# Narrow stationary blocks, four side by side, for the small fp32 products of a linear-attention and feed-forward kernel, and a later first load on ScalarE

## Chip, cores and metric

One core of a Trainium2 chip runs the kernel. The metric is device microseconds of one execution, as the median of several runs. TensorE (PE) multiplies, VectorE (DVE), ScalarE (ACT) and GpSimd (POOL) do the elementwise work, and SyncE (SP) issues most of the loads.

## Reference

For each of 4 batches and 4 heads (sequence 1088, head dimension 32, r = 8) there are quadratic features of queries and keys; the result feeds a feed-forward layer with 2048 hidden units on 4352 tokens of width 128.

```python
a = np.einsum('rd,bhsd->bhsr', S1, x); b = np.einsum('rd,bhsd->bhsr', S2, x)
phi(x) = np.einsum('bhsi,bhsj->bhsij', a, b).reshape(..., r * r)      # 64 features
kv  = np.einsum('bhsf,bhsd->bhfd', phi(k), v)
z   = np.sum(phi(k), axis=2)
x   = (phi(q) @ kv) / (phi(q) . z + 1e-06)        # heads side by side: 128 wide
h   = x @ w_in
g   = where(h >= 1, h, where(h <= -1, 0, (h + 1)**2 / 4))
out = g @ w_out
```

S1, S2, w_in and w_out are 64-bit floats; the kernel turns them into 32-bit parts on chip.

## The kernel before

**Attention, per batch.** The sequence is cut into 9 tiles of 128 tokens. `keys` projects each key tile onto S1 and S2 (`abk`, L432: the key tile is stationary, 128 columns, and the 64 columns of `s_all` move), copies it to SBUF (`ab`, L437), forms the features (`kp`, L442), and sums two things over the tiles in PSUM: the normaliser (`z`, L451: 32 stationary columns, 32 moving) and the key sums (`kv`, L468: two products of 64 stationary and 128 moving columns a tile). The normaliser's diagonal blocks are kept (`zm`, L456), multiplied back by S2 (L458, with `back` stationary) and put into `proj`. `kv` is masked, transposed and copied (`kvm`, L478, `kvb`). `queries` projects query tiles onto `proj` (`abq`, L497: 128 stationary, 96 moving), makes the features divided by the denominator (`as`, `terms`, `den`, `ap`, `qp`), transposes them (`tp`, L528) and gathers (`nd`, L542: two products of 64 stationary columns). `x_hi` and `x_lo` (L548) split the result in two parts for the feed-forward layer. All these products are in plain fp32: the trace has two records, called passes here, for each such matmul of the program (the transposes have one).

**Feed-forward, in 144 units** of up to 512 tokens by 128 hidden columns: three fp32r matmuls up (L584 to L586), an activation on ACT and DVE (L595, L597, L600, L606), a subtraction on POOL (L610), three matmuls down (L620, L621, L624). Each is 512 (or 256) moving columns against 128 stationary ones.

**The order** on each engine comes from `Plan`, which is run when the program is built: every step has a due time, an engine and an assumed cost; at each moment it takes the earliest due step that its own clock thinks is ready. Tile pools give buffers. Where PE has nothing to do before 24 us, it gets a filler: a bf16 product of 512 columns (`wide`, L279) or of 256 (`narrow`, L280). ScalarE issues one load itself, the first chunk of `w_in` (`raw_i`, L325).

Of the kernel before, what the change touches and what calls it, by code (L numbers as in the profile page):

```python
# [63 lines left out]
class Plan:  # L64
# [46 lines left out]
    def run(self):  # L111
# [26 lines left out]
        while left or done:  # L138
# [13 lines left out]
            for e in engines:  # L152
# [21 lines left out]
                    if best[2] is not None and now + best[1].ways[best[2]][1] > soon[1] + 0.05:  # L174
                        continue
                if e == "PE" and best is None and now < self.warm:
                    cost, filler = (0.115, self.narrow) if now > 2.5 else (0.43, self.wide)
                    f = Step(0.0, [("PE", cost, None, (), (), filler)])
                    f.taken, f.start = 0, now
                    order.append(f)  # L180
                    free_at[e] = now + cost
                    heapq.heappush(events, free_at[e])
                    continue
# [72 lines left out]
def tile_kernel(ctx: ExitStack, tc: tile.TileContext, qT, kT, v, S, w_in, w_out, outT):  # L256
# [32 lines left out]
        return Buf("ps", name, [P, 512])  # L289


    ident = cst.tile([P, P], F32, name="ident")
    make_identity(nc, ident)
    mask = cst.tile([P, 2, F], F32, name="mask")
    nc.gpsimd.memset(mask, 0.0)
    for h in range(H):
        nc.gpsimd.memset(mask[h * D : (h + 1) * D, h % 2], 1.0)
    blocks = cst.tile([HR, HR], F32, name="blocks")
    nc.gpsimd.memset(blocks, 1.0)
    nc.gpsimd.affine_select(out=blocks, in_=blocks, compare_op=ALU.is_ge, fill=0.0, base=0,  # L300
                            pattern=[[-R, H], [0, R]], channel_multiplier=1)
    nc.gpsimd.affine_select(out=blocks, in_=blocks, compare_op=ALU.is_ge, fill=0.0, base=R - 1,
                            pattern=[[R, H], [0, R]], channel_multiplier=-1)
# [12 lines left out]
    SC = S.shape[1]  # L316
    s_raw = cst.tile([P, SC, 2], I32, name="s_raw")
    s_all = cst.tile([P, SC], F32, name="s_all")
    back = cst.tile([HR, P], F32, name="back")
    proj = [cst.tile([P, H, 3 * R], F32, name=f"proj{i}") for i in range(2)]  # L320


# [55 lines left out]
            out=lo, in0=of(mag), in1=hi.bitcast(F32), op=ALU.subtract), r=[mag, toks[0]], w=[toks[1]])  # L378

    def weights(due, src, c, hi, lo, tag, due_load=None, lands=None):  # L380
        raw = Buf("raw", f"raw_{tag}{c}", [P, WC, 2], I32)
        load(due - 4 if due_load is None else due_load, src[:, c * WC : (c + 1) * WC, :], raw, P * WC * 8, lands=lands)
        w = slice(c * WC, (c + 1) * WC)
        from_double(due, lambda: of(raw), raw, WC, f"{tag}{c}", hi=hi[:, w], lo=lo[:, w],
                    toks=[(f"{tag}h", c), (f"{tag}l", c)])
# [28 lines left out]
    def keys(b, d):  # L414

        kb, qb, vb = loaded[b]
        front = b == 0
        tag = "h" if front else "at"
        late = 3.0 if front else 0.0
        z = bank(f"z{b}")  # L420
        kp = Buf("kp", f"kp{b}", [P, NTL, H * F])
        abs_ = []
        groups = GRP if front else [range(0, 5), range(5, NTL)]
        for gi, grp in enumerate(groups):
            n = len(grp)
            kt = [kb.part(gi) if front else kb]
            ab = bank(f"abk{b}_{gi}", tag)
            sbuf = Buf("ab", f"ab{b}_{gi}", [P, 2, 5 * H, R])

            def project(ab=ab, grp=grp):  # L430
                for i, t in enumerate(grp):
                    nc.tensor.matmul(of(ab)[:, i * 64 : (i + 1) * 64], lhsT=of(kb)[:, t], rhs=s_all.rearrange("p (c h i) -> p h c i", c=2, h=H),  # L432
                                     start=True, stop=True)

            plan.add(d(0.05 + 0.1 * gi), "PE", n * 0.22, project, r=[*kt, "s_all"], w=[ab])
            view = lambda ab=ab, n=n: of(ab)[:, : n * 64].rearrange("p (m c i) -> p m c i", c=2, i=R)
            plan.add(d(0.1 + 0.1 * gi), "ACT", act(n * 64), lambda sbuf=sbuf, view=view, n=n: nc.scalar.copy(  # L437
                of(sbuf)[:, :, : n * H].rearrange("p c m i -> p m c i"), view()), r=[ab], w=[sbuf])
            pool = front and gi in KP_POOL
            eng = nc.gpsimd if pool else nc.vector  # L440
            plan.add(d(0.15 + 0.1 * gi), "POOL" if pool else "DVE", pool_t(n * 256) if pool else dve(n * 256),
                     lambda sbuf=sbuf, view=view, n=n, grp=grp, eng=eng, pool=pool: eng.tensor_tensor(  # L442
                out=of(kp)[:, grp[0] : grp[-1] + 1].rearrange("p t (h i j) -> p (t h) i j", h=H, i=R),
                in0=of(sbuf)[:, 0, : n * H].unsqueeze(3).broadcast_to([P, n * H, R, R]),
                in1=(of(sbuf)[:, 1, : n * H] if pool else view()[:, :, 1]).unsqueeze(2).broadcast_to([P, n * H, R, R]), op=ALU.mult),
                r=[sbuf] if pool else [ab, sbuf], w=[kp.part(gi)])

            def zsum(sbuf=sbuf, n=n, grp=grp):
                for i, t in enumerate(grp):
                    m = slice(i * H, (i + 1) * H)  # L450
                    nc.tensor.matmul(of(z)[:HR, :HR], lhsT=of(sbuf)[:, 1, m], rhs=of(sbuf)[:, 0, m],  # L451
                                     start=(t == 0), stop=(t == NTL - 1))

            plan.add(d(0.16 + 0.1 * gi), "PE", n * 0.07 + 0.1, zsum, r=[sbuf], w=[z])
        zm = Buf("zm", f"zm{b}", [HR, HR])
        plan.add(d(0.45), "DVE", dve(32), lambda: nc.vector.tensor_tensor(  # L456
            out=of(zm), in0=of(z)[:HR, :HR], in1=blocks, op=ALU.mult), r=[z], w=[zm])
        plan.add(d(0.5), "PE", 0.3, lambda: nc.tensor.matmul(  # L458
            of(z)[:, 64 : 64 + HR], lhsT=back, rhs=of(zm), start=True, stop=True), r=[zm, "back"], w=[z])
        plan.add(d(0.55), "ACT", act(32), lambda: nc.scalar.copy(  # L460
            proj[b % 2][:, :, 2 * R :], of(z)[:, 64 : 64 + HR].rearrange("p (h i) -> p h i", h=H)),
            r=[z], w=[("proj", b % 2)])
        kv = bank(f"kv{b}")

        def sums(grp):
            for t in grp:
                for p in range(2):
                    nc.tensor.matmul(of(kv)[64 * p : 64 * p + 64, :P], lhsT=of(vb)[:, t, 64 * p : 64 * p + 64],  # L468
                                     rhs=of(kp)[:, t, p * P : (p + 1) * P], start=(t == 0), stop=(t == NTL - 1))

        for gi, grp in enumerate(groups):
            vt = [vb.part(0) if front else vb]
            plan.add(d(0.5 + 0.1 * gi) + late, "PE", len(grp) * 0.24 + 0.1, lambda grp=grp: sums(grp),
                     r=[kp.part(gi), *vt], w=[kv])
        kvm = Buf("kvm", f"kvm{b}", [P, 2, F])
        plan.add(d(0.8) + late, "DVE", dve(P), lambda: nc.vector.tensor_tensor(
            out=of(kvm), in0=of(kv)[:, :P].rearrange("p (s f) -> p s f", s=2), in1=mask, op=ALU.mult), r=[kv], w=[kvm])
        plan.add(d(0.85) + late, "PE", 0.11, lambda: nc.tensor.transpose(  # L478
            out=of(kv)[:, P : 2 * P], in_=of(kvm).rearrange("p s f -> p (s f)"), identity=ident), r=[kvm], w=[kv])
        kvb = Buf("kvb", f"kvb{b}", [P, P])  # L480
        copy_to(d(0.9) + late, lambda: of(kvb), lambda: of(kv)[:, P : 2 * P], P, [kv], [kvb])
        return kvb

    def queries(b, kvb, dues):
        _, qb, _ = loaded[b]
        front = b == 0
        for gi, grp in enumerate(QGRP[b]):
# [88 lines left out]
    def unit(u):  # L576
# [55 lines left out]
                     lat=P * n * 4 / 410e3)  # L632


    table = cst.tile([P, 1], F32, name="table")
    plan.add(-50, "ACT", 1.3, lambda: nc.scalar.copy(table, ones[:, :1]), w=["table"])
    load(-30, S, s_raw, P * SC * 8, tok="s_raw")
    load_attn(0, -29, [-28.5, -27], -27.5)
    from_double(-25, lambda: s_raw, "s_raw", SC, "s", whole=s_all, whole_tok="s_all")
    turned = bank("turned")  # L640
    plan.add(-13, "PE", 0.11, lambda: nc.tensor.transpose(
        out=of(turned)[:HR, :P], in_=s_all[:, HR:], identity=ident),
        r=["s_all"], w=[turned])
    plan.add(-13, "ACT", act(P), lambda: nc.scalar.copy(back, of(turned)[:HR, :P]), r=[turned], w=["back"])
# [7 lines left out]
    for u, (c0, n, j) in enumerate(units):  # L652
        first_unit.setdefault(j // JW, u)
    for c in range(DFF // WC):
        weights([I0, I1, first_unit[c] - 6][min(c, 2)], w_in, c, wi_hi, wi_lo, "i", *((None, None) if c else (-40, 4.6)))
        weights([O0, O1, first_unit[c] - 2][min(c, 2)], w_out, c, wo_hi, wo_lo, "o", None if c else -26)
    need = {}
    for b in range(1, B):
# [74 lines left out]
```

## Time and profile before

| | |
|---|---|
| median of 3 runs | 256.61 us (256.57 to 256.63) |
| the profiled execution | 257.05 us, of which the span is 254.9 us |
| granted TensorE clock, mean | 1.0 |
| busy share: PE, PEld, DVE, ACT, POOL | 98, 78, 77, 82, 74% |
| passes of abk, abq, kv, z in the trace | 72, 72, 144, 72 |
| feed-forward matmuls | 864 |

The span is the stretch from the first to the last instruction of the program; 2.15 us of the execution's time lie outside it. A busy engine in the profile may still be waiting within an instruction, and the ends of matmuls are modelled, so starts say more than durations there.

### The profile page before, as it was taken

How to read it: one execution, taken by the hardware profiler on the slowest of the kernel's cores; microseconds unless marked ns; L12 is line 12 of the kernel's file. 1: busy time of each engine (PE TensorE's matmuls, PEld its weight loads, DVE VectorE, ACT ScalarE, POOL GpSimd, SP SyncE). 2: the span in 40 equal slices, each digit the busy share in tenths (PEclk: the TensorE clock that was granted, in tenths of full speed). 3: DMA queues.
4: the chain of work that ended last, by engine and by line, in shares of the span. 5: the costliest groups of instructions: out<-in, count | busy, mean ns of one | idle time of the engine just before them, and what ended most of it. 6: DMA issues, size and time to landing. Idle time of an engine off the chain costs nothing.

```text
span 254.9 us, 4257 instructions
## 1 busy us (share of the span) xinstructions
PE 250.3 (98%) x1408; PEld 199.3 (78%) x1408; DVE 195.0 (77%) x367; ACT 209.6 (82%) x437; POOL 189.8 (74%) x173
## 2 busy tenths in 40 slices
PE   8999999999999999999999999999999999999994
PEld 4877887888678877888788886888788868888883
DVE  2689985897947985894879638986989689738882
ACT  3358999999999768987896649977897789789993
POOL 3424799899878774888687517895889588959992
PEclk9999999999999999999999999999999999999999
DMA  6962239400001300001000100001000100010001
GB/s 221 401 276 82 87 95 378 157 1 0 0 3 41 134 4 0 1 0 41 2 0 0 41 2 0 1 5 41 0 0 3 41 0 0 4 41 1 3 0 62
DMA packets 4773, 13.83 MB, mean 54 GB/s; under 512 B 528, under 2 KB 1168, under 8 KB 4752
## 3 DMA queue, kind: packets, MB, share of 16 engines
q1 hardware_dynamic: 4608, 13.04, 14.0%
q10 hardware_dynamic: 144, 0.52, 0.6%
q8 instruction: 11, 0.18, 0.3%
q14 instruction: 10, 0.08, 0.1%
HBM read 11.34 MB, written 2.23 MB: 53 GB/s over the span
## 4 chain that ended last, share of the span: by engine, by line
PE 92%; ACT 6%; issue 0%; ACTq 0%
PE acc L620 12%; PE acc L624 12%; PE acc L621 12%; PE h L585 12%; PE h L584 12%; PE h L586 12%; PE tp L528 3%; PE abq L497 3%; PE kv L468 3%; PE nd L542 3%; PE abk L432 3%; PE warm L280 2%; ACT s L597 2%; ACT s L595 1%; ACT g_hi L606 1%; PE z L451 1%
## 5 line engine op out<-in xcount | busy, mean ns | idle before, releaser
L610 POOL TENSOR_TENSOR g_lo<-g,g_hi 128x512 fp32r<-128x512 f32 (+1 forms) x140 | 171.5, 1252 | 46.8 <-ACT g_hi L606 21.9
L600 DVE SCALAR_TENSOR_TENSOR g<-h,s 128x512 f32<-128x512 f32 (+1 forms) x144 | 92.7, 657 | 41.2 <-ACT s L597 38.6
L595 ACT ACTIVATE s<-h 128x512 f32<-128x512 f32 (+1 forms) x144 | 79.2, 576 | 19.2 <-PE h L586 18.8
L597 ACT ACTIVATE s<-s 128x512 f32<-128x512 f32 (+1 forms) x144 | 85.1, 616 | 1.1
L620 PE MATMUL acc<-g_hi,wo_hi 128*128 128x512 f32 (+1 forms) x144 | 56.4, 392 | 0.0
L585 PE MATMUL h<-x_lo,wi_hi 128*128 128x512 f32 (+1 forms) x144 | 55.0, 382 | 0.0
L584 PE MATMUL h<-x_hi,wi_hi 128*128 128x512 f32 (+1 forms) x144 | 55.0, 382 | 0.0
L586 PE MATMUL h<-x_hi,wi_lo 128*128 128x512 f32 (+1 forms) x144 | 54.8, 381 | 0.0
L621 PE MATMUL acc<-g_hi,wo_lo 128*128 128x512 f32 (+1 forms) x144 | 54.7, 382 | 0.0
L600 DVE SCALAR_TENSOR_TENSOR g_hi<-h,s 128x512 fp32r<-128x512 f32 (+1 forms) x76 | 49.9, 658 | 1.7 <-PE acc L624 0.7
L624 PE MATMUL acc<-g_lo,wo_hi 128*128 128x512 f32 (+1 forms) x144 | 51.2, 388 | 0.0
L606 ACT CAST g_hi<-g 128x512 fp32r<-128x512 f32 (+1 forms) x68 | 40.1, 593 | 4.0 <-DVE g L600 3.3
L620 PEld LDWEIGHTS acc<-g_hi,wo_hi 128*128 128x128 f32 x144 | 27.2, 189 | 7.3 <-issue 1.7
L624 PEld LDWEIGHTS acc<-g_lo,wo_hi 128*128 128x128 f32 x144 | 26.6, 188 | 7.1 <-issue 1.4
L584 PEld LDWEIGHTS h<-x_hi,wi_hi 128*128 128x128 f32 x144 | 27.0, 188 | 5.8 <-PE nd L542 0.3
L585 PEld LDWEIGHTS h<-x_lo,wi_hi 128*128 128x128 f32 x144 | 27.1, 188 | 5.6
L586 PEld LDWEIGHTS h<-x_hi,wi_lo 128*128 128x128 f32 x144 | 27.0, 188 | 5.5
L621 PEld LDWEIGHTS acc<-g_hi,wo_lo 128*128 128x128 f32 x144 | 27.1, 188 | 5.0
L518 DVE TENSOR_TENSOR qp<-ap,abq 128x768 f32<-128x768 f32 (+1 forms) x13 | 11.5, 888 | 0.2
L442 DVE TENSOR_TENSOR kp<-ab,abk 128x1280 f32<-128x1280 f32 (+2 forms) x8 | 9.8, 1234 | 2.2 <-ACT ab L437 2.2
L528 PE MATMUL tp<-ident,qp 128*128 128x128 f32 x72 | 10.5, 277 | 0.1
L497 PEld LDWEIGHTS abq<-proj,q 128*128 128x128 f32 x72 | 9.2, 191 | 0.9 <-ACT wi_hi L376 0.2
(75 smaller groups left out, 195.4 us busy)
## 6 DMA issues: line engine op xcount, KB each, us to landing
v<-in_v SPq DMA_DIRECT2D x4, 576.0 KB, 6.3
raw_o<-in_w_out SPq DMA_DIRECT2D x4, 512.0 KB, 5.7
outT<-o SPq DMA_DIRECT2D x8, 256.0 KB, 2.0
k<-in_kT SPq DMA_DIRECT2D x3, 576.0 KB, 8.1
q<-in_qT SPq DMA_DIRECT2D x3, 576.0 KB, 7.1
raw_i<-in_w_in SPq DMA_DIRECT2D x3, 512.0 KB, 3.9
k<-in_kT SPq DMA_DIRECT2D x3, 192.0 KB, 4.2
raw_i<-in_w_in ACTq DMA_DIRECT2D x1, 512.0 KB, 4.0
```

Of the source, the lines that this page charges most:

```text
L528: nc.tensor.transpose(out=of(tp)[:, i * P : (i + 1) * P], in_=of(qp)[:, i, p * P : (p + 1) * P], identity=ident)
L584: nc.tensor.matmul(t[:, :n], lhsT=wi_hi[:, fj], rhs=x_hi[:, xs], start=True, stop=False)
L585: nc.tensor.matmul(t[:, :n], lhsT=wi_hi[:, fj], rhs=x_lo[:, xs], start=False, stop=False)
L586: nc.tensor.matmul(t[:, :n], lhsT=wi_lo[:, fj], rhs=x_hi[:, xs], start=False, stop=True)
L595: plan.add(u, "ACT", act(n), lambda: nc.scalar.activation(of(s)[:, :n], of(h)[:, :n], AF.Relu, bias=0.5, scale=0.5), r=[h], w=[s])
L597: plan.add(u, "ACT", act(n, False), lambda: nc.scalar.activation(of(s)[:, :n], of(s)[:, :n], AF.Square), w=[s])
L600: nc.vector.scalar_tensor_tensor(out=of(out)[:, :n], in0=of(h)[:, :n], scalar=1.0, in1=of(s)[:, :n], op0=ALU.max, op1=ALU.min)
L606: plan.add(u, "ACT", act(n, False), lambda: nc.scalar.copy(of(g_hi)[:, :n], of(g)[:, :n]), r=[g], w=[g_hi])
L610: plan.add(u, "DVE" if late else "POOL", dve(n) if late else pool_t(n), lambda: eng.tensor_tensor(out=of(g_lo)[:, :n], in0=of(g)[:, :n], i ...
L620: nc.tensor.matmul(of(acc)[:, :n], lhsT=wo_hi[:, fj], rhs=of(g_hi)[:, :n], start=first, stop=False)
L621: nc.tensor.matmul(of(acc)[:, :n], lhsT=wo_lo[:, fj], rhs=of(g_hi)[:, :n], start=False, stop=False)
L624: nc.tensor.matmul(of(acc)[:, :n], lhsT=wo_hi[:, fj], rhs=of(g_lo)[:, :n], start=False, stop=last)
```

## The change

Four kinds of product are cut into 32 stationary columns each. The key and query projections (`abk`, `abq`) become four matmuls a tile, one for each quarter of the tile's tokens, writing 32 partitions of PSUM each. The key sums become four matmuls a tile, one a head, with 64 moving columns where there were 128 (the blocks that the mask would drop are no longer computed). The normaliser sums keep their shape but write tile t to partitions of quarter t mod 4, so that four partial sums stand side by side; `blocks`, `zm` and `back` grow to 128 partitions, and the product L458 adds the four up. `back` itself is made by four matmuls in place of one transpose. The planner's costs for these steps change with them, the fillers stay 512 columns wide for longer, the step that touched ACT's table first is removed, and ACT's load of the first `w_in` chunk goes into a buffer that POOL writes first, so that it waits for POOL.

```diff
+ABK = 0.13
+ABQ = 0.18
+ZS = 0.04
+KV = 0.15
...
-                    cost, filler = (0.115, self.narrow) if now > 2.5 else (0.43, self.wide)
+                    cost, filler = (0.115, self.narrow) if now > 3.6 else (0.22 if now > 2.6 else 0.43, self.wide)
...
+    raw_i0 = Buf("raw", "raw_i0", [P, WC, 2], I32)
+    nc.gpsimd.memset(of(raw_i0)[:, :1], 0)
...
-    blocks = cst.tile([HR, HR], F32, name="blocks")
+    blocks = cst.tile([P, HR], F32, name="blocks")
+    quarters = [slice(c * HR, (c + 1) * HR) for c in range(P // HR)]
     nc.gpsimd.memset(blocks, 1.0)
...
+    for c in quarters:
+        make_blocks(blocks[c])
...
-        raw = Buf("raw", f"raw_{tag}{c}", [P, WC, 2], I32)
+        raw = raw_i0 if lands is not None else Buf("raw", f"raw_{tag}{c}", [P, WC, 2], I32)
...
-                    nc.tensor.matmul(of(ab)[:, i * 64 : (i + 1) * 64], lhsT=of(kb)[:, t], rhs=s_all.rearrange("p (c h i) -> p h c i", c=2, h=H),
-                                     start=True, stop=True)
-
-            plan.add(d(0.05 + 0.1 * gi), "PE", n * 0.22, project, r=[*kt, "s_all"], w=[ab])
+                    for c in quarters:
+                        nc.tensor.matmul(of(ab)[c, i * 64 : (i + 1) * 64], lhsT=of(kb)[:, t, c],
+                                         rhs=s_all.rearrange("p (c h i) -> p h c i", c=2, h=H), start=True, stop=True)
+
+            plan.add(d(0.05 + 0.1 * gi), "PE", n * ABK, project, r=[*kt, "s_all"], w=[ab])
...
-                    nc.tensor.matmul(of(z)[:HR, :HR], lhsT=of(sbuf)[:, 1, m], rhs=of(sbuf)[:, 0, m],
-                                     start=(t == 0), stop=(t == NTL - 1))
+                    nc.tensor.matmul(of(z)[quarters[t % 4], :HR], lhsT=of(sbuf)[:, 1, m], rhs=of(sbuf)[:, 0, m],
+                                     start=(t < 4), stop=(t + 4 >= NTL))
...
-                for p in range(2):
-                    nc.tensor.matmul(of(kv)[64 * p : 64 * p + 64, :P], lhsT=of(vb)[:, t, 64 * p : 64 * p + 64],
-                                     rhs=of(kp)[:, t, p * P : (p + 1) * P], start=(t == 0), stop=(t == NTL - 1))
+                for h in range(H):
+                    nc.tensor.matmul(of(kv)[quarters[h], :F], lhsT=of(vb)[:, t, quarters[h]],
+                                     rhs=of(kp)[:, t, h * F : (h + 1) * F], start=(t == 0), stop=(t == NTL - 1))
...
-                    nc.tensor.matmul(of(abc)[:, i * 96 : (i + 1) * 96], lhsT=of(qb)[:, t], rhs=pr, start=True, stop=True)
+                    for c in quarters:
+                        nc.tensor.matmul(of(abc)[c, i * 96 : (i + 1) * 96], lhsT=of(qb)[:, t, c], rhs=pr,
+                                         start=True, stop=True)
...
-    table = cst.tile([P, 1], F32, name="table")
-    plan.add(-50, "ACT", 1.3, lambda: nc.scalar.copy(table, ones[:, :1]), w=["table"])
...
+    def turn_back():
+        for c in quarters:
+            nc.tensor.matmul(of(turned)[c, :P], lhsT=s_all[:, HR:], rhs=ident, start=True, stop=True)
...
-        weights([I0, I1, first_unit[c] - 6][min(c, 2)], w_in, c, wi_hi, wi_lo, "i", *((None, None) if c else (-40, 4.6)))
+        weights([I0, I1, first_unit[c] - 6][min(c, 2)], w_in, c, wi_hi, wi_lo, "i", *((None, None) if c else (-40, 5.4)))
```

New costs move steps. On PE, in the first batch, the order between the normaliser's last product and the first transposes was this (`x6` is six matmuls of the program in a row):

```order
L458 MATMUL z_162<-zm_201,back 128x32
L468 MATMUL kv_208<-kp_160,v_118 64x128 x6
L497 MATMUL abq_0_217<-proj_94,q_111 128x96 x2
L468 MATMUL kv_208<-kp_160,v_118 64x128 x6
L497 MATMUL abq_1_235<-proj_94,q_111 128x96 x2
L468 MATMUL kv_208<-kp_160,v_118 64x128 x6
```

After the change, five fillers follow the normaliser's product, and then the same place reads so:

```order
L510 MATMUL abq_0_243<-proj_102,q_116 32x96 x8
L510 MATMUL abq_1_252<-proj_102,q_116 32x96 x8
L480 MATMUL kv_264<-kp_180,v_123 32x64 x12
L284 LDWEIGHTS const-bfloat16-1.0
L284 MATMUL warm<-const-bfloat16-1.0 128x256
L284 LDWEIGHTS const-bfloat16-1.0
L284 MATMUL warm<-const-bfloat16-1.0 128x256
L480 MATMUL kv_264<-kp_180,v_123 32x64 x24
```

Both query projections now stand ahead of the key sums, where each stood behind a part of them. Later on PE, where the third batch's keys meet the feed-forward stream, the order was this:

```order
L624 MATMUL acc_1119<-g_lo_1122,wo_hi 128x512
L497 MATMUL abq_2_1146<-proj_95,q_158 128x96 x3
L432 MATMUL abk_0_1156<-s_all,k_573 128x64 x5
L432 MATMUL abk_1_1175<-s_all,k_573 128x64 x4
L451 MATMUL z_1190<-ab_0_1182 32x32 x5
L620 MATMUL acc_1119<-g_hi_1137,wo_hi 128x512
```

It becomes this, with the normaliser sums moved behind the next eleven feed-forward matmuls, to stand with the key sums:

```order
L638 MATMUL acc_1259<-g_lo_1257,wo_hi 128x512
L510 MATMUL abq_2_1284<-proj_103,q_189 32x96 x12
L444 MATMUL abk_0_1303<-s_all,k_825 32x64 x20
L444 MATMUL abk_1_1334<-s_all,k_825 32x64 x16
L634 MATMUL acc_1259<-g_hi_1275,wo_hi 128x512
```

The number of matmuls in a tile's projection has grown fourfold, and nothing else in this stretch has moved. In the batches after the first, stretches of products with 64 or 32 stationary columns between others with 128, called narrow runs here, number 17 before and 23 after, counted over PE's whole order.

## Rows read from the trace of the kernel before

**Rows 1.** The page: span, busy time and share, and PE's granted clock in 40 slices.
```profile
span 254.9 us, 4257 instructions
...
PE 250.3 (98%) x1408; PEld 199.3 (78%) x1408; DVE 195.0 (77%) x367; ACT 209.6 (82%) x437; POOL 189.8 (74%) x173
...
PEclk9999999999999999999999999999999999999999
```

**Rows 2.** Busy time by stretch: length, then each engine's busy time (instructions), clock, DMA.
```profile
25.00:65.00 40.00, 39.81 (x234) 32.21 (x231) 33.97 (x62) 39.63 (x82) 37.01 (x33) 1.00 0.33 114
65.00:75.00 10.00, 10.00 (x46) 6.85 (x45) 6.72 (x13) 8.94 (x18) 8.67 (x8) 1.00 0.00 0
75.00:250.00 175.00, 175.00 (x944) 141.75 (x943) 137.08 (x249) 146.81 (x305) 134.23 (x112) 1.00 0.04 15
```

**Rows 3.** The chain that ended last, in order of time: start, length, instructions (passes).
```profile
39.78 0.44 PE z L451 x8
...
82.79 0.46 PE acc L624 x2
83.25 0.64 PE abq L497 x6
83.89 1.98 PE abk L432 x18
85.88 0.43 PE z L451 x10
86.31 0.43 PE acc L620
...
91.16 0.37 PE z L451 x8
...
92.33 1.24 PE kv L468 x20
...
93.91 1.02 PE kv L468 x16
94.93 0.43 PE acc L624
...
111.36 0.26 PE acc L624
```

**Rows 4.** Timeline of PE from 11.25 to 11.26 us and from 11.243 to 11.248 us.
```profile
11.25 0.33 PE L468 MATMUL kv<-kp,v 128*64 128x128 f32 x2
11.25 0.32 PE L468 MATMUL kv<-kp,v 128*64 128x128 f32 x1
```

**Rows 5.** Timeline of the first 20 us, rows that the change touches.
```profile
0.79 1.28 ACT L636 ACT_TABLE_LOAD   x1 [0.79 <-PEq L721]
...
0.85 0.38 ACTq L325 DMA_DIRECT2D raw_i<-in_w_in  x1
...
1.31 0.20 POOL L295 MEMSET mask<- 128x128 f32 x1
...
3.22 0.26 ACT L349 ACTIVATE mags<-s_raw 128x64 f32<-128x64 f32 x1 [0.94 <-DMA s_raw<-in_S]
...
7.74 0.67 ACT L349 ACTIVATE magi<-raw_i 128x512 f32<-128x512 f32 x1
8.50 0.61 POOL L351 TENSOR_SCALAR hci<-magi 128x512 f32<-128x512 f32 x1 [5.19 <-ACT magi L349]
...
12.05 0.69 PE L497 MATMUL abq<-proj,q 128*128 128x96 f32 x4
...
13.47 0.69 PE L497 MATMUL abq<-proj,q 128*128 128x96 f32 x4
...
19.49 0.42 DVE L548 TENSOR_TENSOR x_lo<-nd,x_hi 128x256 fp32r<-128x256 f32 x1
...
20.07 0.48 PE L584 MATMUL h<-x_hi,wi_hi 128*128 128x512 f32 x1
```

**Rows 6.** The page's DMA issues: KB each, us from issue to landing.
```profile
raw_i<-in_w_in ACTq DMA_DIRECT2D x1, 512.0 KB, 4.0
```

More of the change, by code (lines that the diff above doesn't have):

```diff
@@ L289, in bank, with make_blocks @@
         return Buf("ps", name, [P, 512])
+    def make_blocks(t):
+        nc.gpsimd.affine_select(out=t, in_=t, compare_op=ALU.is_ge, fill=0.0, base=0,
+                                pattern=[[-R, H], [0, R]], channel_multiplier=1)
+        nc.gpsimd.affine_select(out=t, in_=t, compare_op=ALU.is_ge, fill=0.0, base=R - 1,
+                                pattern=[[R, H], [0, R]], channel_multiplier=-1)
     ident = cst.tile([P, P], F32, name="ident")
     make_identity(nc, ident)
+    raw_i0 = Buf("raw", "raw_i0", [P, WC, 2], I32)
+    nc.gpsimd.memset(of(raw_i0)[:, :1], 0)
     mask = cst.tile([P, 2, F], F32, name="mask")
@@ L297, in tile_kernel @@
         nc.gpsimd.memset(mask[h * D : (h + 1) * D, h % 2], 1.0)
-    blocks = cst.tile([HR, HR], F32, name="blocks")
+    blocks = cst.tile([P, HR], F32, name="blocks")
+    quarters = [slice(c * HR, (c + 1) * HR) for c in range(P // HR)]
     nc.gpsimd.memset(blocks, 1.0)
[L300 to L303, printed above, removed]
+    for c in quarters:
+        make_blocks(blocks[c])
     terms = []
@@ L318, in tile_kernel @@
     s_all = cst.tile([P, SC], F32, name="s_all")
-    back = cst.tile([HR, P], F32, name="back")
+    back = cst.tile([P, P], F32, name="back")
     proj = [cst.tile([P, H, 3 * R], F32, name=f"proj{i}") for i in range(2)]
@@ L450, in zsum @@
                     m = slice(i * H, (i + 1) * H)
-                    nc.tensor.matmul(of(z)[:HR, :HR], lhsT=of(sbuf)[:, 1, m], rhs=of(sbuf)[:, 0, m],
-                                     start=(t == 0), stop=(t == NTL - 1))
-            plan.add(d(0.16 + 0.1 * gi), "PE", n * 0.07 + 0.1, zsum, r=[sbuf], w=[z])
-        zm = Buf("zm", f"zm{b}", [HR, HR])
+                    nc.tensor.matmul(of(z)[quarters[t % 4], :HR], lhsT=of(sbuf)[:, 1, m], rhs=of(sbuf)[:, 0, m],
+                                     start=(t < 4), stop=(t + 4 >= NTL))
+            plan.add(d(0.16 + 0.1 * gi), "PE", n * ZS, zsum, r=[sbuf], w=[z])
+        zm = Buf("zm", f"zm{b}", [P, HR])
         plan.add(d(0.45), "DVE", dve(32), lambda: nc.vector.tensor_tensor(
-            out=of(zm), in0=of(z)[:HR, :HR], in1=blocks, op=ALU.mult), r=[z], w=[zm])
-        plan.add(d(0.5), "PE", 0.3, lambda: nc.tensor.matmul(
+            out=of(zm), in0=of(z)[:, :HR], in1=blocks, op=ALU.mult), r=[z], w=[zm])
+        plan.add(d(0.5), "PE", 0.22, lambda: nc.tensor.matmul(
             of(z)[:, 64 : 64 + HR], lhsT=back, rhs=of(zm), start=True, stop=True), r=[zm, "back"], w=[z])
@@ L466, in sums @@
             for t in grp:
-                for p in range(2):
-                    nc.tensor.matmul(of(kv)[64 * p : 64 * p + 64, :P], lhsT=of(vb)[:, t, 64 * p : 64 * p + 64],
-                                     rhs=of(kp)[:, t, p * P : (p + 1) * P], start=(t == 0), stop=(t == NTL - 1))
+                for h in range(H):
+                    nc.tensor.matmul(of(kv)[quarters[h], :F], lhsT=of(vb)[:, t, quarters[h]],
+                                     rhs=of(kp)[:, t, h * F : (h + 1) * F], start=(t == 0), stop=(t == NTL - 1))
         for gi, grp in enumerate(groups):
             vt = [vb.part(0) if front else vb]
-            plan.add(d(0.5 + 0.1 * gi) + late, "PE", len(grp) * 0.24 + 0.1, lambda grp=grp: sums(grp),
+            plan.add(d(0.5 + 0.1 * gi) + late, "PE", len(grp) * KV, lambda grp=grp: sums(grp),
                      r=[kp.part(gi), *vt], w=[kv])
@@ L476, in keys @@
         plan.add(d(0.8) + late, "DVE", dve(P), lambda: nc.vector.tensor_tensor(
-            out=of(kvm), in0=of(kv)[:, :P].rearrange("p (s f) -> p s f", s=2), in1=mask, op=ALU.mult), r=[kv], w=[kvm])
+            out=of(kvm), in0=of(kv)[:, :F].unsqueeze(1).broadcast_to([P, 2, F]), in1=mask, op=ALU.mult), r=[kv], w=[kvm])
         plan.add(d(0.85) + late, "PE", 0.11, lambda: nc.tensor.transpose(
@@ L496, in project @@
                 for i, t in enumerate(grp):
-                    nc.tensor.matmul(of(abc)[:, i * 96 : (i + 1) * 96], lhsT=of(qb)[:, t], rhs=pr, start=True, stop=True)
-            plan.add(d(0.0), "PE", n * 0.225, project, r=[qb.part(QPART[gi]) if front else qb, ("proj", b % 2)], w=[abc])
+                    for c in quarters:
+                        nc.tensor.matmul(of(abc)[c, i * 96 : (i + 1) * 96], lhsT=of(qb)[:, t, c], rhs=pr,
+                                         start=True, stop=True)
+            plan.add(d(0.0), "PE", n * ABQ, project, r=[qb.part(QPART[gi]) if front else qb, ("proj", b % 2)], w=[abc])
             view = lambda abc=abc, m=m: of(abc)[:, : m * 24].rearrange("p (m c i) -> p m c i", c=3, i=R)
@@ L640, in tile_kernel @@
     turned = bank("turned")
[L641 to L644, printed above, removed]
+    def turn_back():
+        for c in quarters:
+            nc.tensor.matmul(of(turned)[c, :P], lhsT=s_all[:, HR:], rhs=ident, start=True, stop=True)
+    plan.add(-13, "PE", 0.25, turn_back, r=["s_all"], w=[turned])
+    plan.add(-13, "ACT", act(P), lambda: nc.scalar.copy(back, of(turned)[:, :P]), r=[turned], w=["back"])
     for i in range(2):
```

## Prediction

> **What bounds the kernel now.** I first read the page [rows 1]: PE is busy for 250.3 of 254.9 us at a granted clock of full speed in all 40 slices, and no other engine is over 82%. Busy time alone doesn't prove a bound, so I then read the chain that ended last [rows 3]. From 39.78 us to the end it is PE with itself: a feed-forward matmul every 0.23 us (two take 0.46), and between them the small fp32 products, each piece starting where the one before ends. What PE spends on a small product there is paid in full, and what it saves is got back in full, as long as the other engines keep up. That condition I read by stretch [rows 2]: from 25 to 65 us ACT is busy for 39.63 of 40 us, so it is as full as PE; from 65 to 75 it has 1.06 us of 10 to spare, and from 75 to 250 us 28.2 of 175. So a gain in the batches whose small products lie after 75 us is safe, and one before 65 us is not. Before 20.07 us, where the first feed-forward matmul starts [rows 5], PE fills its time with dummies, and a chain over several engines sets the pace.
>
> **What a small product costs now, from the chain [rows 3].** A pass with 128 stationary columns takes 0.11 us whatever moves: 18 of `abk` take 1.98, 6 of `abq` 0.64. For `kv`, 20 passes take 1.24 and 16 take 1.02: 0.055 each, and about 0.14 once. For `z`, 10 take 0.43 and 8 take 0.37: 0.03 each, and 0.13 once. So a tile costs 0.22 (`abk`, two passes), 0.21 (`abq`), 0.22 (`kv`, four) and 0.06 (`z`, two): 0.71 us together.
>
> **Why `kv` is the row that the new products resemble.** Its two halves write different halves of the partitions. The timeline [rows 4] shows one record within 5 ns of the stretch's start, 0.32 us long, and two by 10 ns later that together last 0.33: they run side by side. A pair then comes every 0.11 us (two times 0.055), which is the pace of 128 moving columns in one pair, and the weight loads of both hide under it. So two narrow blocks really work at once. Four of them I have not seen: that is the unknown of this change.
>
> If four go side by side as two do, a round of four passes lasts as long as one pair's moving columns: 0.11 x 64/128 = 0.055 us for `abk` and `kv`, 0.11 x 96/128 = 0.083 for `abq`. A tile needs two rounds: 0.11, 0.11 and 0.165 in place of 0.22, 0.22 and 0.21. For `z` the four groups overlap too; the tile lies between 0.015 (a quarter) and 0.06 (no gain), and I take 0.03. The saving is 0.11 + 0.11 + 0.05 + 0.03 = 0.30 us a tile. Batches 1 to 3 have 27 tiles: 8.1 us.
>
> The other end of the bound is the `z` row: 0.03 us a pass when every pass has 32 stationary columns, in a single column group. If that pace holds for four groups too, a tile takes 8 x 0.03 = 0.24 for each of the three products and 0.06 for `z`, 0.78 in all: a loss of 0.07 a tile, 1.9 us. I take the first, because the rows that show more than one group at work are those of `kv`, and there the second product followed the first by 10 ns or less, far under 30.
>
> A rule of the Trainium skill ("TensorE: Matmul & The Clock Gate", Part 3) speaks against this: a weight load overlaps matmuls in flight only where the row groups differ, and here all four blocks span all rows. By it each round would add its weight load to the moving columns, and the savings of `abq` would vanish. The trace does not agree for two blocks: the pair's pace of 0.11 us leaves no room for a load between.
>
> **Switching, which the change adds.** After `z` and after `kv` the first feed-forward matmul takes 0.43 in place of 0.23, after `abq` only 0.26 (the row at 111.36) [rows 3]. With the 0.13 to 0.14 that the narrow run itself has once, each narrow run among wide products costs about 0.34 us on top of its work; a run of 128-column fp32 products costs 0.03. `abk` and `abq` now become narrow. Runs in batches 1 to 3 grow from 17 to 23, fewer than one might fear, since projections stand next to each other or to `z`, and `z` next to `kv`: 6 x 0.34 = 2.0 us back. For a lone group of three `abq` tiles it is a plain loss: 0.64 + 0.03 before, 0.50 + 0.34 after.
>
> **The head.** The projections of batch 0 shorten too, but what matters is when the first feed-forward matmul starts, at 20.07, which waits for `x_lo` of the second query group (19.49 + 0.42) [rows 5]. That group's projection started at 13.47, behind two thirds of the key sums; now it comes right behind the first group's, ahead of all key sums. With nothing else moving, the first group's 12.05 would come about 0.9 us earlier (half of the key projections' two microseconds and the 0.6 of key sums ahead of it, less switches and a wait that fillers placed in advance may keep), and the second group's 13.47 then about 2 us. Between them and `x_lo` stand DVE's chains and the conversion of the first weights, which don't shrink. Bounds 0 and 2 us; I take 1.0.
>
> **Edits that I cost at nothing.** ScalarE's first load was issued at 0.85 and landed 4.0 us later [rows 5, 6]; it will wait for POOL's identity matrix and a tiny fill in the place of the mask's at 1.31, so it is issued near 1.5 and lands near 5.5. Its first reader is at 7.74: 2 us of cover. Queued behind it on ACT is the table load, 1.28 us from 0.79 to 2.07, now some 1.5 to 2.8; its first user starts at 3.22, 0.4 us of cover. Without that cover the price is 0.65 us at the head. POOL's six more block selections lie before its first work at 8.50, ahead of which it idles 5.19 us [rows 5]. The removed table copy was on ACT, in the same empty time. The `kvm` mask, `zm` and `back` keep their free sizes or halve them, and one product with 128 stationary columns stays one.
>
> **ScalarE's limit.** Batch 1's keys and queries run before 65 us. Their share is 9 x 0.30 = 2.7, less four more narrow runs at 0.34: 1.3 us net. ACT is full there; PE's stock of finished inputs may give half of it. I take 0.65 as lost.
>
> **Sum:** 8.1 - 2.0 + 1.0 - 0.65 = 6.45 us. The profiled execution of 257.05 (span 254.9) becomes 250.6 (span 248.45); it lies 0.44 over the median of the runs, so for the median 256.61 - 6.5 = 250.1 us.
>
> **Rivals.**
> 1. *A floor on issue.* A pass may need a least distance p from the next, whatever the groups; a tile then has 26 of them (3 x 8 + 2). With p between 0.014 (8 passes in 0.11) and 0.03, the tiles save 27 x (0.71 - 26p). At p = 0.02 that is 5.1, less 2.0, plus some 0.7 at the head and less 0.3 for ACT: 253.1 us. At p = 0.025 it is 1.6, less 2.0, plus 0.4 for a slighter head: 256.6. For it: no row shows more than two passes within 0.1 us kept up over a long run. Against it: the 10 ns of [rows 4]. The Trainium skill ("TensorE: Matmul & The Clock Gate", on the issue floor) has start-to-start never below about 25 ns, which would put this rival at no change; the pair of [rows 4] is nearer than that, though it is two starts and not a stream.
> 2. *ScalarE, and POOL behind it, become the bound.* Not only batch 1 is lost (1.3 us), but about half of what the later batches give (8.1 - 2.0 - 1.3 = 4.8). For it: the full 25 to 65 us and POOL's 37.0 of 40 there. Against it: 28 us of room after 75. 256.6 - 1.0 - 2.4 = 253.2 us.
> 3. *Blocks follow one another* at the pace of the `z` row, p = 0.03: the tiles lose 1.9 us, the narrow runs cost 2.0, and the head loses some 0.3 in its longer projections: 260.8 us, slower. The point of decision is where 27 x (0.71 - 26p) equals the 2.0 for switching: p = 0.0245. Against it: [rows 4].
> 4. *The savings and the switches cancel*, with narrow runs dearer than I read them (0.34 is from `z` and `kv`, not from these): 6 us of savings would need 1 us a run. Little speaks for it.
>
> **How the numbers follow.** The forecast, four blocks side by side with PE still the bound, gets 0.61; its own range is 248 to 252 us, from the head's 0 to 2 and ACT's part. Rival 1 gets 0.14, most of it in 252 to 256, rival 2 0.14, rival 3 0.08, rival 4 0.03. A measurement of this kernel can tell 0.2%, 0.5 us, from no change. Faster: 0.61 + 0.14 + 0.10 of rival 1 = 0.85. Same: 0.02 of rival 1 and rival 4's 0.03: 0.05. Slower: 0.08 and 0.02 of rival 1: 0.10. The range from 247.5 to 254.5 leaves out rival 3 and part of rival 1, and a little at the low end.
>
> **What would show it.** In the chain, `abk` at about 0.055 us for each round of four, 36 matmuls in about 1 us where 18 passes took 1.98; `kv` 16 matmuls of a batch's last group in about 0.6; the first feed-forward matmul after `abq` at 0.43 in place of 0.26; the first one of all near 19 us; ACT still near 40 of 40 from 25 to 65. If single passes of a tile stand 25 to 30 ns apart, rival 1 or 3 is right; if PE shows idle time before `acc` with ACT or POOL as its releaser, rival 2. I would be most wrong if `kv`'s two halves share something that four blocks can't.

## The result, and the profile after

The changed kernel takes 249.43 us (median of 4 runs, 248.79 to 250.24) beside 256.62 us (256.57 to 256.75) for the kernel before: a ratio of 0.972, with a 95% interval of 0.969 to 0.975. The forecast was 250.1 us. Its profiled execution is the longest of the four: 250.24 us, with a span of 248.5. The page of the changed kernel, in the lines of [rows 1]:

```profile
span 248.5 us, 5408 instructions
...
PE 240.1 (97%) x1986; PEld 186.9 (75%) x1986; DVE 192.2 (77%) x363; ACT 210.3 (85%) x440; POOL 191.4 (77%) x180
...
PEclk9999999989999999999999999999999999999999
```

PE is busy for 10 us less, but the span shrinks by only 6.4: PE now waits, and one slice of the clock is below full. The stretches show where; the first three answer to [rows 2], and the last two cut out the place.

```profile
25.00:65.00 40.00, 37.10 (x340) 27.95 (x328) 32.29 (x59) 37.82 (x78) 36.22 (x32) 0.96 0.31 114
65.00:75.00 10.00, 10.00 (x47) 6.94 (x46) 6.44 (x12) 9.23 (x18) 9.18 (x8) 1.00 0.01 2
75.00:245.00 170.00, 170.00 (x1261) 136.94 (x1259) 135.79 (x247) 148.29 (x310) 135.04 (x112) 1.00 0.04 16
...
49.00:53.55 4.55, 2.65 (x10) 1.54 (x10) 3.07 (x7) 3.10 (x6) 2.78 (x4) 1.00 1.02 419
53.55:57.00 3.45, 3.02 (x8) 1.78 (x7) 3.45 (x9) 3.45 (x8) 2.57 (x3) 0.51 0.41 170
```

PE is again busy all the time after 65 us, but only for 37.10 of the 40 us before (39.81 in [rows 2]). Within that, the granted clock is 0.51 from 53.55 to 57.0 us.

The chain that ended last, in the places that answer to [rows 3]:

```profile
44.71 5.59 DMA raw_o<-in_w_out
...
83.67 0.63 PE abq L510 x24
84.30 1.00 PE abk L444 x72
85.31 0.43 PE acc L634
...
88.02 0.21 PE z L463 x9
88.23 0.58 PE kv L480 x38
88.82 0.07 PE z L463 x6
88.89 0.43 PE acc L638
...
93.32 0.58 PE kv L480 x32
...
106.92 0.63 PE abq L510 x24
107.55 0.43 PE acc L634
```

Nine tiles of `abk` take 1.00 us in 72 passes, where 18 passes took 1.98. Four tiles of `kv` take 0.58 where they took 1.02. The lone `abq` group of three tiles takes 0.63, about as before (0.64), and the matmul behind it now 0.43 in place of 0.26. The new row is the first: a load that lasts 5.59 us is part of the chain.

The timeline, in the rows that answer to [rows 4 to 6], and from 44 us those of the wait:

```profile
1.44 0.38 ACTq L336 DMA_DIRECT2D raw_i<-in_w_in  x1
...
1.85 1.28 ACT L360 ACT_TABLE_LOAD   x1 [1.85 <-POOL mask L307]
...
3.14 0.26 ACT L360 ACTIVATE mags<-s_raw 128x64 f32<-128x64 f32 x1
...
5.20 0.33 PE L444 MATMUL abk<-s_all,k 128*32 128x64 f32 x4
...
7.48 0.69 ACT L360 ACTIVATE magi<-raw_i 128x512 f32<-128x512 f32 x1
...
10.42 0.87 PE L510 MATMUL abq<-proj,q 128*32 128x96 f32 x32
...
17.57 0.42 DVE L562 TENSOR_TENSOR x_lo<-nd,x_hi 128x256 fp32r<-128x256 f32 x1
...
18.17 0.48 PE L598 MATMUL h<-x_hi,wi_hi 128*128 128x512 f32 x1
...
43.96 0.68 DVE L373 SCALAR_TENSOR_TENSOR magi<-raw_i,mi 128x512 int32<-128x512 int32 x1
...
44.71 0.33 SPq L340 DMA_DIRECT2D raw_o<-in_w_out  x1
...
50.39 0.68 ACT L360 ACTIVATE mago<-raw_o 128x512 f32<-128x512 f32 x1 [2.11 <-DMA raw_o<-in_w_out]
...
50.72 0.40 PE L635 MATMUL acc<-g_hi,wo_lo 128*128 128x512 f32 x1
52.99 0.50 PE L598 MATMUL h<-x_hi,wi_hi 128*128 128x512 f32 x1 [1.87 <-DVE g L614]
```

The row at 5.20 comes from the stretch 5.19 to 5.24 us: four passes, one for each quarter, start in it, 6 to 7 ns apart by their records, and the next four follow 0.09 us later. The first and second query groups follow each other directly at 10.42, and the first feed-forward matmul starts 1.90 us earlier than before. At 50.39 ACT has waited 2.11 us for the last chunk of `w_out`, whose buffer DVE freed only at 44.64; PE then waits 1.87 us for what is queued behind it.

**Where the lead goes.** In both traces, and in those of all experiments, every one of the 864 feed-forward matmuls is recorded, so one can ask how far ahead each kernel is at a given matmul. The 201st is a good point: by then each kernel has done the same small products, those of batches 0 and 1 without batch 1's last query group, and none of the third batch's. Starts in us; all rows but the first are differences from the first.

| kernel | first | 201st | last | from the 201st to the last |
|---|---|---|---|---|
| before | 20.07 | 80.77 | 251.12 | 170.35 |
| changed | -1.90 | +0.47 | -6.31 | -6.78 |
| e1, same quarter in a row | -0.70 | +3.80 | +6.74 | +2.94 |
| e2, wide queries | -1.70 | -2.33 | -7.95 | -5.62 |
| e3, four raw buffers | -1.61 | -1.23 | -8.04 | -6.81 |
| e4, load and table step alone | -0.28 | -0.94 | -2.60 | -1.66 |
| e5, 64-byte tile | -0.47 | -0.53 | -0.84 | -0.31 |
| e6, changed, old places | -1.81 | -0.75 | -5.69 | -4.94 |
| e8, key sums alone | -0.91 | -0.97 | -2.91 | -1.94 |
| e9, old planner costs | -1.60 | -0.94 | -5.23 | -4.29 |
| e10, 128-byte tile | -0.45 | -0.64 | -1.43 | -0.79 |
| e11, wide queries, four buffers | -1.83 | -2.56 | -8.15 | -5.59 |
| e12, the same, less on ScalarE | -1.97 | -2.49 | -8.33 | -5.84 |
| e13, 4096-byte tile | -0.11 | -0.44 | -2.18 | -1.74 |

In the changed kernel's trace all of the head's lead, and all that batch 1 saves, is gone at the 201st matmul. Everything it keeps comes later. The first column is good to about half a microsecond: e5, e10 and e13 run the same order of instructions as the kernel before, and their first matmul comes 0.11 to 0.47 us earlier; the traced execution of the kernel before is itself 0.44 us longer than its median.

### The profile page after: what moved, and what is told of

Read it like the earlier page. It is cut to its first block, busy times and chain, and to the rows that moved or that the text cites. A ratio compares the mean times of both kernels' runs of the same rounds, so it can differ in the third digit from the quotient of the medians.

```text
span 248.5 us, 5408 instructions
## 1 busy us (share of the span) xinstructions
PE 240.1 (97%) x1986; PEld 186.9 (75%) x1986; DVE 192.2 (77%) x363; ACT 210.3 (85%) x440; POOL 191.4 (77%) x180
## 4 chain that ended last, share of the span: by engine, by line
PE 76%; ACT 16%; DMA 4%; DVE 1%; issue 1%; SPq 0%; ACTq 0%
PE acc L638 11%; PE acc L634 11%; PE acc L635 11%; PE h L598 10%; PE h L599 10%; PE h L600 10%; ACT s L611 5%; ACT s L609 5%; ACT g_hi L620 3%; PE nd L556 3%; PE tp L542 2%; DMA raw_o<-in_w_out 2%; PE abq L510 2%; DMA k<-in_kT 2%; PE kv L480 2%; PE abk L444 1%
## 5 line engine op out<-in xcount | busy, mean ns | idle before, releaser
L598 PE MATMUL h<-x_hi,wi_hi 128*128 128x512 f32 (+1 forms) x144 | 55.6, 386 | 2.3 <-DVE g L614 1.9
L542 PEld LDWEIGHTS tp<-ident,qp 128*128 128x128 f32 x72 | 8.3, 140 | 2.3 <-DVE g L614 0.8
```

Source lines behind the costliest of these rows:

```text
L542: nc.tensor.transpose(out=of(tp)[:, i * P : (i + 1) * P], in_=of(qp)[:, i, p * P : (p + 1) * P], identity=ident)
L598: nc.tensor.matmul(t[:, :n], lhsT=wi_hi[:, fj], rhs=x_hi[:, xs], start=True, stop=False)
```

## Experiments

**e1: the four passes of a tile in another order.** The loops over quarters and over tiles are exchanged, so that successive passes write the same quarter (shown once for the projections, which have it for keys and for queries, and once for the key sums).

```diff
-                for i, t in enumerate(grp):
-                    for c in quarters:
+                for c in quarters:
+                    for i, t in enumerate(grp):
...
-            for t in grp:
-                for h in range(H):
+            for h in range(H):
+                for t in grp:
```

> The changed kernel, in which the four quarters of a tile no longer follow each other: all tiles of a group for the first quarter, then all for the second, and so on (projections and key sums). Same products, same order of steps. Theory, side by side only because neighbours in the order write different quarters: a tile of abk and kv then takes 8 passes of 0.055 = 0.44 us in place of 0.11, abq 8 x 0.083 = 0.66 in place of 0.165, for 27 tiles 27 x (0.33 + 0.33 + 0.5) = 31 us, so 275 to 282 us. Rival, the engine looks far enough ahead to pair quarters up anyway: within 1 us of 249.4.

Measured: 263.24 us (ratio 1.026, 1.024 to 1.028), between the two. The chain of its trace, at the same place:

```profile
87.00 0.95 PE abq L510 x20
...
88.18 2.39 PE abk L444 x67
...
93.52 1.49 PE kv L480 x37
```

An `abk` pass now takes 2.39/67 = 0.036 us in place of 0.014, a `kv` pass 0.040 in place of 0.015. The instructions are the same, and the kernel is slower than the one before. So the gain isn't in the narrow shape but in neighbours that use different quarters. The starts in the trace show why it is not as slow as expected: within one quarter they are 55 to 56 ns apart, as the forecast has it for a whole round of four (0.055 us), but where one quarter gives way to the next, passes of both alternate, 6 to 50 ns apart, so that neighbouring quarters still overlap in part.

**e2: the query projections left at 128 columns.**

```diff
-ABQ = 0.18
+ABQ = 0.225
...
-                    for c in quarters:
-                        nc.tensor.matmul(of(abc)[c, i * 96 : (i + 1) * 96], lhsT=of(qb)[:, t, c], rhs=pr,
-                                         start=True, stop=True)
+                    nc.tensor.matmul(of(abc)[:, i * 96 : (i + 1) * 96], lhsT=of(qb)[:, t], rhs=pr, start=True, stop=True)
```

> The changed kernel with the query projection back as one product of 128 stationary columns a tile, at its old planner cost. Theory of the prediction: 27 x 0.05 = 1.35 us more work, about five narrow runs of 0.34 us fewer, a head longer by some 0.3: 249.4 us, give or take 0.7. Rival, narrow runs cost nothing and the query projection's part of the gain is real: 250.8 us or more.

Measured: 248.64 us (0.969, 0.968 to 0.970), at the low end of what was expected. Narrow queries bring nothing here. From the 201st matmul on they are worth 6.78 - 5.62 = 1.16 us, but with wide ones the kernel is further ahead by then, in an order that the planner made anew: from 20 to 70 us PE waits 0.6 us in all, where it waits 2.9 in the changed kernel's trace. Which of the order's differences does that was not tried.

**e3: a fourth buffer for raw chunks of weights**, so that the late load starts earlier (`raw=3` becomes `raw=4`).

> The changed kernel with a fourth buffer for raw weights, so that the last w_out load can be issued before the third buffer is read out. Theory, the idle PE between 49 and 57 us and the fall of the clock come from that load, which landed at 50.3 us with ScalarE waiting for it: 245.5 to 246.5 us, with no idle stretch of PE over 0.4 us after 25 us. Rival, ScalarE and POOL are full up to 65 us and would stop PE anyway: 248.5 to 249.4 us, with the idle time spread.

Measured: 248.34 us (0.968, 0.966 to 0.969), nearer to the rival. Its timeline:

```profile
32.69 0.33 SPq L340 DMA_DIRECT2D raw_o<-in_w_out  x1
...
55.02 0.50 PE L598 MATMUL h<-x_hi,wi_hi 128*128 128x512 f32 x1 [1.16 <-DVE magi L373]
```

The load now starts 12 us earlier and ACT no longer waits for it, yet PE waits 1.16 us at 55.02. By the medians the late load costs about 1.1 us (249.43 - 248.34), but one of the changed kernel's four runs is the profiled one with the fallen clock; how long the load takes varies (see e6). The rest of the lost lead has another cause. It can be read where the load is out of the way, in e3's stretch from 25 to 65 us and in its chain:

```profile
25.00:65.00 40.00, 37.95 (x356) 28.98 (x356) 33.62 (x61) 39.94 (x83) 38.12 (x33) 1.00 0.28 101
...
61.20 0.53 ACT s L611
61.73 0.38 ACT qpT L401
62.16 0.70 DVE g L614
...
62.90 0.55 PE tp L542 x3
```

ACT is busy for 39.94 of the 40 us and PE for 37.95. The chain runs over ACT until 62.11 us and comes to PE only at 62.90. In the changed kernel it comes to PE at 64.61, in e6 at 63.16. In the kernel before it did so at 39.78 [rows 3], from this piece:

```profile
39.47 0.27 ACT ab L437
```

**e4: the later first load and the removed table step alone**, with all products as before.

> The kernel before with one part of the change alone: ScalarE's first load waits for POOL, and the step that touched the table is gone. Theory of the prediction, both hidden: 256.6 us within 0.3, first feed-forward matmul at 20.1 us. Rival, the first keys' earlier arrival gives part of the head's 1.9 us: 255.6 us or less.

Measured: 254.40 us (0.991, 0.990 to 0.993): 2.2 us faster. That is the rival's number but not its reason, since the head is only 0.28 us earlier. The gain lies where nothing was changed: 512-column feed-forward matmuls that follow each other directly (starts less than 260 ns apart) start 228.7 ns apart on average, where they start 232.2 ns apart before. The changed kernel has 228.8. With the 4-byte tile `table` gone, all buffers allocated behind it lie 32 bytes lower, `g_hi` and `g_lo` among them. Four experiments move only such places.

**e5, e10, e13: the kernel before, buffers shifted.** `table` is widened to 64, 128 and 4096 bytes; the order on every engine stays the same.

```diff
-    table = cst.tile([P, 1], F32, name="table")
+    table = cst.tile([P, 16], F32, name="table")
...
```

> The kernel before, with one change: the small tile `table` is 64 bytes wide in place of 4, so that all buffers that come after it in its pool begin at a multiple of 64 bytes, where they began 32 bytes behind one. The order of instructions on each engine is the same. Theory (the place of the buffers sets the pace of the feed-forward matmuls): spacing falls from about 232 to about 228 ns and the time from 256.6 to 253.5 to 254.5 us, as in the load-only run (254.40), though its head is not changed. Rival (the pace in that run came from its order or its first load): no change, 256.6 us within 0.5.

> The kernel before, with the tile `table` 128 bytes wide, so that all later buffers begin at a multiple of 128 bytes (32 bytes behind one before, 64 bytes behind one with the 64-byte tile; 0 in the changed kernel and in each experiment that showed the fast spacing of feed-forward matmuls). The order on each engine is that of before. Theory (the places modulo 128 bytes set the spacing): 229 ns in place of 232, 253.0 to 254.5 us. Rival (the fast spacing comes with the missing table step or some other place): 256.4 us within 0.4, as with the 64-byte tile.

> The kernel before, with the tile `table` 4096 bytes wide: later buffers (features, activations, `g_hi`, `g_lo`) begin at the same places modulo 4096 as in the changed kernel, and at the very addresses of the four-buffer experiment; the order on each engine is that of before, the table step included. Theory (places alone set the spacing of feed-forward matmuls, with a period longer than 128 bytes): 229 ns, as in every kernel without the table tile, and 253.0 to 254.5 us. Rival (the fast spacing needs the table step gone, or a first load that waits): about 231 ns or more, 255.3 us or more.

Measured: 256.35 us (0.9988, 0.9979 to 0.9997), 255.51 (0.996, 0.994 to 0.997) and 254.83 (0.992, 0.991 to 0.994), with mean spacings of 231.5, 230.7 and 228.8 ns. So my guesses of a multiple of 64 and of 128 bytes fell. The last one, at the changed kernel's places modulo 4096, has the fast spacing, with the table step in place. The same 44 matmuls, first and last start, in the timeline of the kernel before:

```profile
100.24 0.48 PE L620 MATMUL acc<-g_hi,wo_hi 128*128 128x512 f32 x1
...
110.33 0.39 PE L621 MATMUL acc<-g_hi,wo_lo 128*128 128x512 f32 x1
```

and in that of e13:

```profile
99.69 0.48 PE L620 MATMUL acc<-g_hi,wo_hi 128*128 128x512 f32 x1
...
109.60 0.39 PE L621 MATMUL acc<-g_hi,wo_lo 128*128 128x512 f32 x1
```

10.09 us become 9.91.

**e6: the changed kernel, shifted back** by an unused 4-byte tile; the order is the same.

```diff
+    cst.tile([P, 1], F32, name="pad")
```

> The changed kernel, with an unused tile of 4 bytes in a pool of its own constants, so that all later buffers begin 32 bytes behind a multiple of 64, as in the kernel before; nothing else differs. Theory (the place of the buffers): spacing of feed-forward matmuls back at about 232 ns, 251.5 to 252.5 us in place of 249.4. Rival (something else about the changed kernel gave the faster pace): 249.4 us within 0.5.

Measured: 251.03 us (0.979, 0.977 to 0.981), a little under what was expected, spacing 232.1 ns. The places are thus worth 1.6 us in the changed kernel (251.03 - 249.43) and 1.7 in the one before (256.56 - 254.83). Its trace also shows the late load once more, in the chain and on ACT, and then PE's waits from 20 to 70 us (total, times, longest):

```profile
44.81 4.01 DMA raw_o<-in_w_out
...
48.91 0.69 ACT L360 ACTIVATE mago<-raw_o 128x512 f32<-128x512 f32 x1 [0.51 <-DMA raw_o<-in_w_out]
...
PE h L598 <- DVE magi L373: 1.2, 1, 1.2
PE tp L542 <- DVE g L614: 0.6, 1, 0.6
PE h L598 <- DVE g L614: 0.3, 1, 0.3
```

The load starts as late as in the changed kernel, but lasts 4.01 us in place of 5.59, and ACT waits 0.51 in place of 2.11. PE's waits come to 2.1 us; in e3, where the load is early, they are nearly the same (1.2, 0.5 and 0.3).

**e8: the key sums alone narrow**, on top of e5.

```diff
-                for p in range(2):
-                    nc.tensor.matmul(of(kv)[64 * p : 64 * p + 64, :P], lhsT=of(vb)[:, t, 64 * p : 64 * p + 64],
-                                     rhs=of(kp)[:, t, p * P : (p + 1) * P], start=(t == 0), stop=(t == NTL - 1))
+                for h in range(H):
+                    nc.tensor.matmul(of(kv)[32 * h : 32 * h + 32, :F], lhsT=of(vb)[:, t, 32 * h : 32 * h + 32],
+                                     rhs=of(kp)[:, t, h * F : (h + 1) * F], start=(t == 0), stop=(t == NTL - 1))
...
-            plan.add(d(0.5 + 0.1 * gi) + late, "PE", len(grp) * 0.24 + 0.1, lambda grp=grp: sums(grp),
+            plan.add(d(0.5 + 0.1 * gi) + late, "PE", len(grp) * 0.15, lambda grp=grp: sums(grp),
...
```

> The kernel before with buffers shifted to multiples of 64 bytes, and of the change itself only the key sums (four products of 32 stationary and 64 moving columns a tile in place of two of 64 and 128). Theory (term by term as predicted: 27 tiles at 0.11 us, no new narrow runs, part of batch 1's share lost on ACT): 2.0 to 3.0 us less than the shifted kernel alone beside it. Rival (what the key sums save is mostly given back in waits on ACT and DVE): less than 1 us less.

Measured: 253.98 us (0.990, 0.989 to 0.992), 2.4 us less than e5 beside it, inside the 2.0 to 3.0 expected. Its chain has the same two pieces as [rows 3], at 0.70 and 0.58 us in place of 1.24 and 1.02:

```profile
91.36 0.70 PE kv L468 x40
...
92.39 0.58 PE kv L468 x32
```

**e9: the planner's old costs** with the narrow products (`ABK`, `ABQ`, `ZS`, `KV` at 0.22, 0.225, 0.095, 0.265).

> The changed kernel with the planner's costs of the small products as they were (0.22, 0.225, 0.095 and 0.265), so that the products are narrow and the planner does not know it. Theory (the gain is the products' own time, not the new order): 248.5 to 250.5 us. Rival (a good part of the gain, or of the loss between 49 and 57 us, comes from the order that the new costs make): outside these bounds, above 251.5 if the order gave the gain, under 248 if it made the loss.

Measured: 251.75 us (0.981, 0.980 to 0.983), so the rival holds: 2.3 us of the gain (251.75 - 249.43) come with the new costs. With the old ones the planner counts on long projections and puts the normaliser's products so close behind them that PE waits for ACT's copy and DVE's mask. PE's waits in this trace, from 80 to 250 us (total, times, longest):

```profile
PE z L470 <- DVE zm L468: 1.0, 2, 0.6
PE z L463 <- ACT ab L449: 0.8, 2, 0.5
```

In the changed kernel PE waits for nothing in this stretch. Another such wait, of 1.27 us, lies at 36 us in the trace of e9, where ACT sets the pace anyway (it is busy for 19.97 of the 20 us from 25 to 45).

**e11 and e12: e2 and e3 together, and then less for ScalarE** (`HI_ACT` from 0.8 to 0.7, which gives more copies to DVE).

> The changed kernel with the query projections again 128 columns wide, and with a fourth buffer for the raw weight chunks. If the two gains seen alone (0.8 and 1.1 us) are of different things, they add up: 247.0 to 247.8 us. Rival (both only ease the same full stretch of ScalarE, VectorE and GpSimd from 45 to 60 us): 248.2 to 248.8 us, no better than either alone.

> The same with fewer copies of `g_hi` on ScalarE in the first 32 units (0.7 in place of 0.8, the rest by VectorE). Theory (ScalarE alone is the full engine from 25 to 45 us, and VectorE has 3.5 us of room there): 0.3 to 0.8 us less than the kernel beside it. Rival (VectorE is full where PE waits, from 50 to 60 us, so the work only changes its place): the same within 0.3 us, or more.

Measured: 248.62 us (0.969, 0.967 to 0.970) and 248.48 (0.968, 0.967 to 0.969). Both rivals hold: the gains of e2 and e3 don't add up, and moving copies to DVE changes nothing that can be told from zero. With four buffers, wide queries (248.62) are no better than narrow ones (e3, 248.34), so e2's lead over the changed kernel is not a price of narrow queries as such. A reason lies in e12's stretch from 45 to 65 us:

```profile
45.00:65.00 20.00, 19.78 (x95) 14.83 (x94) 18.96 (x37) 19.89 (x42) 19.69 (x19) 1.00 0.03 13
```

ACT has 19.89, POOL 19.69 and DVE 18.96 of 20 us: three engines are full there, not one. No version's median is under 248.3 us.

## Why the forecast was right

**Four blocks side by side: right in mechanism and size.** The step from the two halves of `kv` to four quarters held. A tile of `abk` takes 1.00/9 = 0.11 us as forecast, and a fifth tile of `kv` adds 0.70 - 0.58 = 0.12 in e8, where the forecast has 0.11. The rule that was weighed in the prediction (the Trainium skill, "TensorE: Matmul & The Clock Gate", Part 3) would add a weight load to each round. The Trainium skill's issue floor ("TensorE: Matmul & The Clock Gate", Part 1) has about 25 ns between starts. The trace doesn't agree with either: 72 passes in 1.00 us are 14 ns each, 0.056 us a round. Rivals 1 and 3 are refuted for this order of passes, while e1 shows that a pass takes 0.036 us on average, even more than rival 3's 0.03, when most neighbours share a quarter.

**Switching: right.** 0.63 us for the lone query group and 0.43 for the next matmul come to 0.83 over a feed-forward matmul's own 0.23; the forecast had 0.50 + 0.34. At a saving of 0.05 us a tile, narrow `abq` earns such a switch back only in long groups, and e2 and e11 show that in sum it earns nothing that can be told.

**After 80 us: right.** For batches 2 and 3 the terms give 18 x 0.30 = 5.4, with 3 x 0.05 = 0.15 for batch 1's last query group, less 2 x 0.34 = 0.7 for the two new narrow runs there: 4.9 us. From the 201st matmul to the last e6, with the places of before, gains 4.94, and the changed kernel less the places (e13) 6.78 - 1.74 = 5.04. Counted from start to start in the traces, `kv` gives 2.12 of the 4.94 (forecast 1.98), `abk` 1.81 (1.98), `z` 1.07 (0.54) and `abq` 0.44 (1.05), while the feed-forward matmuls take 0.66 more (the switches, 0.7): the sum is right partly because `z` and `abq` miss by like amounts in opposite directions.

**The head: mis-sized.** I took 1.0 and it gave 1.90 (1.81 in e6) by the trace of the kernel before. By those of e5, e10 and e13, which have that kernel's order, it gave 1.4 to 1.8. Both groups' projections came earlier than I allowed, at 10.42 in place of 12.05 and 13.47. The edits costed at nothing there did cost nothing: the load was issued at 1.44 and landed 4.5 us later by the page, before 7.48, and the table load, though late, ended at 3.13, just before its user at 3.14. The cover was used up there: S had landed 1.8 us after its issue at 0.80, at 2.6, and its user waited for the table load; before it landed 2.4 us after, at 3.2. In e4, with load and table step alone, the head is 0.28 us earlier, which is within the spread of unchanged heads.

**ScalarE's limit: the step that failed.** I took 0.65 as lost, half of batch 1's net gain, and counted the head's gain in full, though the prediction itself calls a gain before 65 us not safe. The chain was PE's own from 39.78 us on; in the changed kernel it runs mainly over ACT until about 63 us (e3, e6), and what PE saves ahead of that comes back only as far as ACT allows. With 1.81 at the head (e6) and 1.15 for batch 1 (the 1.3 forecast less the 0.15 of its last query group), about 3.0 us of lead reach that stretch; at the 201st matmul 0.75 are left in e6, so 2.2 were lost, and PE's waits of 2.1 us in e6 are of that size. In the changed kernel's profiled execution more than the whole lead was. How much is lost depends on the order: with e2's the lead grew in the same stretch, from 1.70 to 2.33 us. Rival 2 had the place right and its reach wrong: nothing is lost after 80 us. One part of the profiled loss was in no rival: the new order frees a buffer later, so the last `w_out` chunk starts at 44.71 and not at 36.85 as before. e3 puts that at about 1.1 us by the medians, but e6, with the load as late and landing sooner, has e3's waits, so this price is not settled.

**No term at all: the places of buffers.** The removed 4-byte tile is worth 1.6 to 1.7 us. I had costed the step as an instruction on ACT and not as a shift of memory. So the forecast's 6.5 us and the measured 7.2 lie close partly by luck, because misses offset each other: about 1.55 us more lost on ACT, against 0.4 to 0.9 more at the head, 0.1 to 0.2 more after 80 us and 1.6 from the places. Without the places, e6's 251.03 is what the terms should have given.

## What to carry to other kernels

Small fp32 products gained here from being cut into narrow blocks only when successive passes went to different blocks, and the planner had to be told the new costs, or it turned part of the gain into waits. A saving on PE counts only where the chain still runs over PE after the change: ask at each point what the other engines still allow, and which buffers' release the new order delays. When an edit adds or removes even a tiny tile, compare the places of everything allocated behind it, and test the same shift on the old kernel before crediting the edit.

## What the runs showed of the hardware

- The spacing of 512-column feed-forward matmuls depends on where other buffers lie: 232.2, 231.5, 230.7 and 228.8 ns with the same order and buffers shifted by 0, 32, 96 and 4064 bytes. Even matmuls whose own operands (`x_hi`, `wi_hi`, allocated ahead of the shifted tile) hadn't moved differed: 230.9 and 232.9 ns with shifts of 0 and 32, 229.0 with 4064. Which buffers and what period matter stays open.
- After PE's wait of 1.87 us before 52.99 us, the granted clock fell to 0.51, the lower level of 1.2 GHz, from 53.55 to 57.0 us, and matmuls started 0.40 to 0.43 us apart in place of 0.23. In e6, whose longest wait was 1.16 us, the clock stayed at 1.00 in this place. The profiled execution is the longest of the four; its mean clock is 0.992, that of the others 0.999 to 1.000.
- Passes of one block (32 columns, 64 moving) start 55 to 56 ns apart, and four passes of four blocks share that time, 6 to 7 ns apart with 36 ns to the next four (e1; the third batch's keys in the changed kernel).
